# Attention scores in eight array tiles of 32 queries instead of four of 64, and one masked copy instead of two

## The chip, the cores and the metric

The kernel runs on one core of one Trainium2 chip. A core has five engines that work side by side: TensorE (PE, matrix products), VectorE (DVE), ScalarE (ACT), GpSimd (POOL) and SyncE (SP, which here issues the transfers). The metric is the time of one execution on the device in microseconds, as the median of several runs. The kernel before takes 720.04 us, the median of 3 runs (719.09 to 720.98).

## The reference

Four sequences of 768 positions with 8 heads of 64 dimensions go through attention in which a query sees the last 128 positions up to itself (the window) and the first 4 positions of the sequence (the sinks). What comes out goes through a feed-forward block of 2048 hidden units.

```python
scores = scale * np.matmul(q, k.transpose(0, 1, 3, 2))
rel = pos[:, None] - pos[None, :]
in_window = (rel >= 0) & (rel < int(window))
keep = is_sink | in_window
scores = np.where(keep, scores, -1000000000.0)
scores = scores - np.max(scores, axis=-1, keepdims=True)
a = np.exp(scores)
a = a / (np.sum(a, axis=-1, keepdims=True) + 1e-09)
return np.matmul(a, v).astype(np.float32)
# then, on all 3072 rows of 512:
h = x @ w_in
sp = np.maximum(h, 0.0) + np.log1p(np.exp(-np.abs(h)))
g = h * erf(sp)
return (g @ w_out).astype(np.float32)
```

## The kernel before, in words

The work is cut into 12 groups of 256 queries (three a sequence), and a group's attention into four steps, one for each pair of heads: 48 steps, numbered s. A group's 256 queries are two blocks of 128, i = 0 and 1. The feed-forward block of a group (lines 761 to 822) runs as 16 blocks f of 128 hidden units; its matmuls fill PE while the attention of later groups is worked in between.

A step goes through these stages: `load` and `prep` bring queries and keys into `kq` with the 64 dimensions of head 0 on partitions 0 to 63 and those of head 1 on partitions 64 to 127; `score` (lines 369 to 428) makes the exponentials; `norm` divides by the sums; `ptrans`, `pread` and `phalf` turn the probabilities round (from step 15 on by way of DVE's transpose and DRAM) and POOL cuts them into halves by the diagonal (line 522); `av` (line 563) multiplies with the values; `xfin` copies out.

In `kq` a row holds, for a pair of heads, three stretches of 144 columns (`KB` = 128 keys of a block and 16 columns for the sinks): the previous block, block 0 and block 1; then the two blocks of queries. A query of block i needs the end of the previous block's keys, the sinks, and the beginning of its own block's. So a contiguous run of columns of `kq`, beginning in the previous block and ending in the own one, covers what a set of neighbouring queries sees.

In `score` the queries of a block are taken in two halves of 64 (`lo`, `hi`). For each half and each head there is one float32 matmul (line 404) of 64 dimensions by 64 queries by 208 keys (`lo`) or 224 keys (`hi`). The float32 matmul is two passes on PE, each with a load of its weights and a record of its own. Two heads lie in the two row halves of the array and write two PSUM banks; two halves of the queries lie in its two column halves and write the two halves of the partitions. Where a group is the first of its sequence, block 0 has no previous block and its runs are 144 columns.

The runs are put into the bank so that the own block's key t stands `KB` columns (or, for `hi`, a like distance) beside the previous block's key t. Of these two a query sees exactly one, as the window is 128 long. Two predicated copies on DVE (line 417), one for `lo` and one for `hi`, each over both heads and both blocks, copy the own block's scores over the previous block's under a triangle `tri` of 64 x 64. After that 144 columns hold all that the softmax needs; a custom DVE operation (line 422) adds the mask and takes the minimum of the negated scores, ScalarE makes the exponential (line 426).

The order of work is not fixed by the loops alone. Every piece is emitted with a priority (`at`, the offsets in `O`), and a planner with a cost model writes out each engine's queue from priorities and modelled times; `follow` ties two instructions of one engine in order. The matmuls of one `score` call are tied one behind another, and from step 17 on the scores follow the attention output of step s - 2 in one burst. A feed-forward block's projection onto the output comes `LAG` = 4 blocks after its hidden layer and activation.

The bank for the scores comes from the pool `ps_s`, which has one buffer of two banks; step 1 uses `ps_h` tiles, step 2 `ps_o` tiles.

Of the kernel before, what the change touches and what calls it, by code (L numbers as in the profile page):

```python
# [9 lines left out]
F32 = mybir.dt.float32  # L10
# [4 lines left out]
ALU = mybir.AluOpType  # L15
# [4 lines left out]
P = 128  # L20
# [19 lines left out]
NE, AL = 4, 2  # L40
# [22 lines left out]
def kernel(  # L63
# [11 lines left out]
    nc = tc.nc  # L75
# [11 lines left out]
    KB, S3 = P + SW, 6 * SW  # L87
# [31 lines left out]
    def set_flags(behind):  # L119
# [3 lines left out]
        behind(nc.vector.tensor_scalar(flag[:, 3:4], eff[0:1, 1:2], float(P), None, op0=ALU.is_le))  # L123
        nc.vector.tensor_reduce(flag1, flag, axis=AX.X, op=ALU.min)
        nc.vector.tensor_copy(flagi, flag1)
# [12 lines left out]
    def fast_path():  # L138
        with ExitStack() as st:
            pers = st.enter_context(tc.tile_pool(name="pers", bufs=1))  # L140
# [7 lines left out]
            ps_s = st.enter_context(tc.tile_pool(name="ps_s", bufs=1, space=PSUM))  # L148
# [6 lines left out]
            rf = work.tile([P, 512], F32, tag="u", bufs=UB, name="rf")  # L155
# [25 lines left out]
            set_mask(mask0)  # L181
            set_mask(mask1)

            tri = pers.tile([P, 64], mybir.dt.int8, name="tri")
            nc.vector.tensor_scalar(tri[:64], rf[:64, :64], float(P), None, op0=ALU.is_ge)
            nc.vector.tensor_scalar(tri[64:], rf[64:, 64:128], float(P), None, op0=ALU.is_lt)

# [6 lines left out]
            sinks = dram.tile([B * NPAIR, P // 2, 2, 2, D], F32, tag="sinks", bufs=1, name="sinks")  # L196

            pst = pers.tile([P, RING, 2, 2, KB], F32, name="pst")

            xp, early = {}, {}  # L200

# [5 lines left out]
            lo, hi = slice(0, HP), slice(HP, P)  # L207
# [122 lines left out]
            def follow(prev, ins):  # L330

                if prev is not None:
                    tc.add_manual_dep(
                        ins.ins, prev.ins.name,
                        mybir.DependencyInfo(mybir.DependencyClass.NoSync, mybir.DependencyReason.DATA), reason="order",
                    )
                return ins
# [22 lines left out]
            def core(s):  # L360

                prev = mark.get(("p", s - 1)) if s - AL == 3 * NPAIR - 1 else None
                late = s - AL >= 2 * NPAIR and s - AL != 3 * NPAIR - 1
                if late:
                    prev = av(s - AL)
                if s < NSTEP:
                    score(s, prev)

            def score(s, prev):

                g, c = divmod(s, NPAIR)
                gb = g % GPB
                d = stp[s]
                d["sum"] = small.tile([P, 2, 2], F32, tag="sum", name=f"sum_{s}")
                d["neg"] = small.tile([P, 2, 2], F32, tag="neg", name=f"neg_{s}")

                ps, both = [], None
                for h in range(2):
                    nm = f"ps_{s}_{h}"
                    if s == 1:  # L380
                        ps.append(ps_h.tile([P, 2, GT], F32, tag="h", name=nm).rearrange("p a t -> p (a t)"))
                    elif s == 2:
                        ps.append(ps_o.tile([P, DM], F32, tag="o", name=nm))
                    else:
                        if both is None:
                            both = ps_s.tile([P, 2, 512], F32, tag="s", name=f"ps_{s}")
                        ps.append(both[:, h, :])


                dx = KB + 80  # L390
                X = [80, 80 + dx]
                for i in range(2):
                    qt = kq[:, c, 3 + i, :]
                    kt = kq[:, c].rearrange("p n t -> p (n t)")
                    runs = ((lo, KB * i, KB + 64, X[i]), (hi, KB * i + 64, KB + 80, X[i] - 80))
                    if gb + i == 0:
                        runs = ((lo, KB, KB, X[i]), (hi, KB, KB, X[i]))
                    for hf, r0, n, x in runs:
                        for h in (1, 0):
                            r = slice(64 * h, 64 * h + 64)  # L400
                            with at(pos(s), "rest") if s >= TT + AL else nullcontext():
                                prev = follow(
                                    prev,
                                    nc.tensor.matmul(ps[h][hf, x : x + n], qt[r, hf], kt[r, r0 : r0 + n], start=True, stop=True),
                                )

                i0 = int(gb == 0)
                for hf, x, y in ((lo, X[0], X[0] + KB), (hi, X[0] + 64, X[0] - 80)):
                    for t in (both,) if both is not None else ps:
                        t = t if both is not None else t.rearrange("p (h t) -> p h t", h=1)  # L410
                        n = t.shape[1]
                        o, w = (
                            t[hf, :, z : z + 2 * dx].rearrange("p h (i t) -> p h i t", i=2)[:, :, i0:, e : e + 64]
                            for z, e in ((min(x, 64), x - min(x, 64)), (min(y, 64), y - min(y, 64)))
                        )
                        mk = tri[hf].rearrange("p (a b t) -> p a b t", a=1, b=1).broadcast_to([64, n, 2 - i0, 64])
                        nc.vector.copy_predicated(o, mk, w)
                for i in range(2):
                    mk = mask if gb > 0 else (mask0, mask1)[i]
                    for h in range(2):  # L420
                        y = pst[:, s % RING, i, h, :]
                        mark["t", s] = nc.vector.tensor_tensor_reduce(  # L422
                            out=y, in0=ps[h][:, X[i] : X[i] + KB], in1=mk, scale=-scale, scalar=3.0e38, op0=ALU.add, op1=ALU.min,
                            accum_out=d["neg"][:, i, h : h + 1],
                        )
                        mark["e", s] = nc.scalar.activation(  # L426
                            y, y, AF.Exp, bias=d["neg"][:, i, h : h + 1], scale=-1.0, accum_out=d["sum"][:, i, h : h + 1]
                        )
# [155 lines left out]
            def at(a, what):  # L584

                key = int(a * PW) + O[what] + (E.get(what, 0) if a < EA else 0)
                return tc.high_priority(offset=tc.tile_snap_priority() + 1 - key)

            def pos(s):

                return s if s < NE else 3 * s - 6 if s < 2 * NPAIR else 4 * s - 12

            plan = {}
            for s in range(NSTEP + AL):
# [23 lines left out]
                if s < 2 * NPAIR:  # L618
                    x = pos(s) + (3 if s < NE else 5)
# [22 lines left out]
            for n in range(32):  # L642
                x = n - 16
# [68 lines left out]
            for m in range(-LEAD, NG * NF + LAG + 2):  # L712
                a = m + LEAD
                live = 0 <= m < NG * NF
                if live:
                    g, f = divmod(m, NF)
# [6 lines left out]
                w = m - LAG  # L723
                if 0 <= w < NG * NF:
# [3 lines left out]
                    if f2 == NF - 1:  # L728
                        for i in range(2):
                            r0 = (g2 * 2 + i) * P  # L730
# [93 lines left out]
    def general_path():  # L824

        NT_S = S // P
        with ExitStack() as st:
# [7 lines left out]
            with tc.tile_pool(name="g_one0", bufs=1) as one, tc.tile_pool(name="g_work0", bufs=2) as work:  # L835
# [16 lines left out]
                with tc.For_i(0, B * H, 1) as bh:  # L852
# [14 lines left out]
                    for i in range(NT_S):  # L867
# [14 lines left out]
                        mx = work.tile([P, 2], F32, tag="mx", name=f"g_mx{i}")  # L882
                        nc.vector.tensor_reduce(mx[:, 0:1], p, axis=AX.X, op=ALU.max)
                        nc.vector.tensor_scalar_mul(mx[:, 0:1], mx[:, 0:1], -1.0)
# [14 lines left out]
            with tc.tile_pool(name="g_one1", bufs=1) as one, tc.tile_pool(name="g_work1", bufs=2) as work:  # L899
# [3 lines left out]
                with tc.For_i(0, B, 1) as b:  # L903
                    for gb in range(GPB):
# [25 lines left out]
                        for i in range(2):  # L930
# [3 lines left out]
                            )  # L934

    fast_path()
    ok = nc.values_load(flagi[0:1, 0:1], min_val=0, max_val=1)
    with tc.If(ok == 0):
# [31 lines left out]
```

## Time and profile before

| | |
|---|---|
| median of 3 runs | 720.04 us (719.09 to 720.98) |
| the profiled execution | 719.41 us, span 717.4 us |
| PE busy | 689.5 us (96%), 5515 passes |
| PE weight loads busy | 568.2 us (79%) |
| DVE busy | 549.4 us (77%) |
| ACT busy | 493.6 us (69%) |
| POOL busy | 299.1 us (42%) |
| granted PE clock, mean | 0.993 |

The span runs from the first to the last instruction of the profiled execution; the execution's own time is a little more. Busy times of PE are those of overlapping passes, so a busy PE may still be waiting for its own pipeline. Rows of the trace name a group of instructions by the line of the kernel, the engine, the operation, and the tile written and read (`ps<-kq`); `x16` is a count.

### The profile page before, as it was taken

Reading aid. Unit: us, or ns where it says so; the run is one execution under the profiler, and the core shown is the slowest. Engines: PE = TensorE matmul, PEld = TensorE weight load, DVE = VectorE, ACT = ScalarE, POOL = GpSimd, SP = SyncE. Lnnn points to the kernel's source line nnn. Section 1 sums busy time; section 2 is a strip of 40 time slices with the busy share of each in tenths; the row PEclk is TensorE's granted clock in tenths of the full one; section 3 lists DMA queues with packets and bytes.
Section 4 is the critical chain, followed back from the end, with each engine's and each line's share of the span. In section 5 each row is a group of like instructions: output and inputs, shape, how many; then the busy total and the mean of one; then the engine's idle time right before and its main releaser. Section 6 shows DMA issues by size and latency. Waiting matters only on the chain. (4 is left out here: it accounts for less than half of the span.)

```text
span 717.4 us, 16155 instructions
## 1 busy us (share of the span) xinstructions
PE 689.5 (96%) x5515; PEld 568.2 (79%) x5515; DVE 549.4 (77%) x1473; ACT 493.6 (69%) x1157; POOL 299.1 (42%) x501
## 2 busy tenths in 40 slices
PE   6779999999999999999999999999999999999997
PEld 3566557688887888788788888888888888889885
DVE  6979997687789888788888588688698687754352
ACT  4777676986984867476677586586677577586572
POOL 3412400234444546454554444555554437342221
PEclk9999999999999999999999999999999999999999
DMA  6999410302216454543553363463463543220001
GB/s 159 283 320 344 168 27 5 78 16 46 66 34 118 102 117 100 127 104 72 124 118 72 65 135 74 87 136 75 95 124 72 102 96 71 44 68 1 30 1 35
DMA packets 246858, 70.10 MB, mean 98 GB/s; under 512 B 214704, under 2 KB 238896, under 8 KB 246768
## 3 DMA queue, kind: packets, MB, share of 16 engines
q1 hardware_dynamic: 246208, 68.92, 41.1%
q8 instruction: 46, 0.75, 0.4%
q14 instruction: 44, 0.36, 0.2%
q10 hardware_dynamic: 560, 0.07, 0.1%
HBM read 50.27 MB, written 18.42 MB: 96 GB/s over the span
## 5 line engine op out<-in xcount | busy, mean ns | idle before, releaser
L770 PE MATMUL h<-xh,wt 128*128 128x256 f32 x1408 | 275.1, 284 | 0.8 <-DVE u L792 0.7
L770 PEld LDWEIGHTS h<-xh,wt 128*128 128x128 f32 x1408 | 223.7, 188 | 15.4 <-issue 8.2
L770 PE MATMUL h<-xl,wt 128*128 128x256 f32 x704 | 197.3, 281 | 0.0
L800 POOL TENSOR_TENSOR g<-u,g 128x512 fp32r<-128x512 f32 x84 | 113.9, 1356 | 181.3 <-DVE g L799 160.1
L788 ACT ACTIVATE u<-r 128x512 f32<-128x512 f32 x288 | 163.1, 622 | 19.2 <-DMA out_dram<-ot 5.3
L792 DVE SCALAR_TENSOR_TENSOR u<-u,u 128x512 f32<-128x512 f32 x168 | 136.6, 813 | 14.0 <-ACT u L788 1.6
L770 PEld LDWEIGHTS h<-xl,wt 128*128 128x128 f32 x704 | 132.1, 188 | 7.0 <-issue 2.8
L815 PE MATMUL o<-wt,g 128*128 128x512 f32 x336 | 134.1, 399 | 0.5 <-DVE g L799 0.5
L816 PE MATMUL o<-wt,g 128*128 128x512 f32 x336 | 132.8, 395 | 0.0
L817 PE MATMUL o<-wt,g 128*128 128x512 f32 x336 | 129.8, 397 | 0.6 <-POOL g L800 0.4
L426 ACT ACTIVATE pst<-pst,neg 128x144 f32<-128x144 f32 x192 | 77.4, 405 | 61.0 <-DVE neg L422 60.7
L792 DVE SCALAR_TENSOR_TENSOR u<-u,h 128x512 f32<-128x512 f32 x84 | 56.8, 676 | 54.9 <-ACT u L788 53.1
L783 ACT ACTIVATE r<-h 128x512 f32<-128x512 f32 x96 | 56.8, 592 | 51.0 <-PE h L770 42.8
L522 POOL TENSOR_SCALAR_AFFINE_SELECT pz<-pa 64x256 f32<-64x256 f32 (+1 forms) x96 | 47.1, 491 | 70.0 <-ACT pa L484 68.9
L815 PEld LDWEIGHTS o<-wt,g 128*128 128x128 f32 x336 | 63.0, 187 | 14.6 <-ACT u L788 1.3
L817 PEld LDWEIGHTS o<-wt,g 128*128 128x128 f32 x336 | 61.7, 187 | 16.0 <-POOL g L800 1.4
L816 PEld LDWEIGHTS o<-wt,g 128*128 128x128 f32 x336 | 63.0, 188 | 10.8 <-issue 0.3
L785 ACT ACTIVATE r<-r 128x512 f32<-128x512 f32 x96 | 60.6, 631 | 2.8
L784 ACT ACTIVATE r<-r 128x512 f32<-128x512 f32 x96 | 60.6, 631 | 2.6
L799 DVE CAST g<-u 128x512 fp32r<-128x512 f32 x84 | 37.4, 445 | 27.3 <-PE o L817 24.1
L513 POOL COPY pz<-pa 64x256 f32<-64x256 f32 x66 | 31.5, 477 | 55.4 <-DMA pa<-pd 54.6
L522 POOL TENSOR_SCALAR_AFFINE_SELECT pa<-pa 64x256 f32<-64x256 f32 (+1 forms) x96 | 50.4, 525 | 4.9
(99 smaller groups left out, 916.6 us busy)
## 6 DMA issues: line engine op xcount, KB each, us to landing
pd<-turn SPq DMA_DIRECT2D x33, 320.0 KB, 2.6
pa<-pd SPq DMA_DIRECT2D x132, 80.0 KB, 2.6
ws<-in_moe_w_in_dram SPq DMA_DIRECT2D x16, 512.0 KB, 6.1
ws<-in_moe_w_out_dram SPq DMA_DIRECT2D x16, 512.0 KB, 8.5
out_dram<-ot SPq DMA_DIRECT2D x24, 256.0 KB, 2.4
v<-in_v_dram SPq DMA_DIRECT2D x56, 96.0 KB, 2.5
kq<-in_k_dram SPq DMA_DIRECT2D x144, 32.0 KB, 2.0
kq<-in_q_dram SPq DMA_DIRECT2D x144, 32.0 KB, 2.2
```

The lines of the kernel that those rows point to most:

```text
L426: mark["e", s] = nc.scalar.activation(y, y, AF.Exp, bias=d["neg"][:, i, h : h + 1], scale=-1.0, accum_out=d["sum"][:, i, h : h + 1])
L522: nc.gpsimd.affine_select(out=out, in_=x, pattern=[[0, 2], [0, 2 - i0], [-sg, HP]], compare_op=op, fill=0.0, base=0, channel_multiplier=sg,)
L770: last = nc.tensor.matmul(o, wt[NC * j + c][:, p, fs], xt[e][:, c, :], start=(m == 0), stop=(m == len(ops) - 1))
L783: nc.scalar.activation(r, h, AF.Tanh, bias=b_t, scale=0.5)
L784: nc.scalar.activation(r, r, AF.Square, bias=b_v, scale=-0.5)
L785: nc.scalar.activation(r, r, AF.Square, bias=b_r)
L788: sq = nc.scalar.activation(u, r, AF.Square, bias=b_a[i], scale=CS)
L792: pr = nc.vector.scalar_tensor_tensor(out=acc, in0=u, scalar=CC[i] * CS**2, in1=x, op0=ALU.add, op1=ALU.mult)
L800: nc.gpsimd.tensor_tensor(gl, acc, gh.bitcast(F32), op=ALU.subtract)
L815: behind(nc.tensor.matmul(o, gh[:, ws], wt[16 + f][:, 0, :], start=(f == 0), stop=False))
L816: nc.tensor.matmul(o, gh[:, ws], wt[16 + f][:, 1, :], start=False, stop=False)
L817: nc.tensor.matmul(o, gl[:, ws], wt[16 + f][:, 0, :], start=False, stop=(f == NF - 1))
```

## The change

The queries of a block are taken in four sets of 32 instead of two of 64, so that a matmul has 64 dimensions, 32 queries and 176 keys (`KB + 32`). A block has eight matmuls instead of four, in eight tiles of the array: two row halves by four column quarters. All sets of a block use one layout in the bank, with the own block's key t always 144 columns behind the previous block's key t; block 1 begins at column 240. Therefore one predicated copy over 128 partitions and 128 columns, under a triangle of 128 x 128, takes the place of the two over 64 partitions. What a set of 32 rows doesn't write is under the copy or outside of the triangle. The bank tile is allocated once for all steps, and in steps 0, 1, 2 and 4 (`NE`) the runs are widened so that no column that the copy reads was never written.

```diff
--- before.py
+++ after.py
@@ -181,9 +181,8 @@
             set_mask(mask0)
             set_mask(mask1)
 
-            tri = pers.tile([P, 64], mybir.dt.int8, name="tri")
-            nc.vector.tensor_scalar(tri[:64], rf[:64, :64], float(P), None, op0=ALU.is_ge)
-            nc.vector.tensor_scalar(tri[64:], rf[64:, 64:128], float(P), None, op0=ALU.is_lt)
+            tri = pers.tile([P, P], mybir.dt.int8, name="tri")
+            nc.vector.tensor_scalar(tri, rf[:, :P], float(P), None, op0=ALU.is_ge)
 
 
 
@@ -196,6 +195,8 @@
             sinks = dram.tile([B * NPAIR, P // 2, 2, 2, D], F32, tag="sinks", bufs=1, name="sinks")
 
             pst = pers.tile([P, RING, 2, 2, KB], F32, name="pst")
+
+            score_banks = ps_s.tile([P, 2, 512], F32, tag="s", name="ps")
 
             xp, early = {}, {}
 
@@ -382,39 +383,40 @@
                     elif s == 2:
                         ps.append(ps_o.tile([P, DM], F32, tag="o", name=nm))
                     else:
-                        if both is None:
-                            both = ps_s.tile([P, 2, 512], F32, tag="s", name=f"ps_{s}")
+                        both = score_banks
                         ps.append(both[:, h, :])
 
 
-                dx = KB + 80
-                X = [80, 80 + dx]
+                X = [0, 240]
                 for i in range(2):
                     qt = kq[:, c, 3 + i, :]
                     kt = kq[:, c].rearrange("p n t -> p (n t)")
-                    runs = ((lo, KB * i, KB + 64, X[i]), (hi, KB * i + 64, KB + 80, X[i] - 80))
-                    if gb + i == 0:
-                        runs = ((lo, KB, KB, X[i]), (hi, KB, KB, X[i]))
-                    for hf, r0, n, x in runs:
+                    for j in range(0, P, 32):
+                        r0, n, x = KB * i + j, KB + 32, X[i] + j
+                        if s in (0, 1, 2, NE):
+                            n = max(n, X[1] + 32 * i - j)
+                        if gb + i == 0:
+                            r0, n, x = KB, KB, X[i]
                         for h in (1, 0):
                             r = slice(64 * h, 64 * h + 64)
                             with at(pos(s), "rest") if s >= TT + AL else nullcontext():
                                 prev = follow(
                                     prev,
-                                    nc.tensor.matmul(ps[h][hf, x : x + n], qt[r, hf], kt[r, r0 : r0 + n], start=True, stop=True),
+                                    nc.tensor.matmul(
+                                        ps[h][j : j + 32, x : x + n], qt[r, j : j + 32], kt[r, r0 : r0 + n], start=True, stop=True
+                                    ),
                                 )
 
                 i0 = int(gb == 0)
-                for hf, x, y in ((lo, X[0], X[0] + KB), (hi, X[0] + 64, X[0] - 80)):
-                    for t in (both,) if both is not None else ps:
-                        t = t if both is not None else t.rearrange("p (h t) -> p h t", h=1)
-                        n = t.shape[1]
-                        o, w = (
-                            t[hf, :, z : z + 2 * dx].rearrange("p h (i t) -> p h i t", i=2)[:, :, i0:, e : e + 64]
-                            for z, e in ((min(x, 64), x - min(x, 64)), (min(y, 64), y - min(y, 64)))
-                        )
-                        mk = tri[hf].rearrange("p (a b t) -> p a b t", a=1, b=1).broadcast_to([64, n, 2 - i0, 64])
-                        nc.vector.copy_predicated(o, mk, w)
+                for t in (both,) if both is not None else ps:
+                    t = t if both is not None else t.rearrange("p (h t) -> p h t", h=1)
+                    n = t.shape[1]
+                    o, w = (
+                        t[:, :, z : z + 2 * X[1]].rearrange("p h (i t) -> p h i t", i=2)[:, :, i0:, e : e + P]
+                        for z, e in ((0, 0), (32, KB - 32))
+                    )
+                    mk = tri.rearrange("p (a b t) -> p a b t", a=1, b=1).broadcast_to([P, n, 2 - i0, P])
+                    nc.vector.copy_predicated(o, mk, w)
                 for i in range(2):
                     mk = mask if gb > 0 else (mask0, mask1)[i]
                     for h in range(2):
```

## Rows read from the trace of the kernel before

**Rows 1.** Busy time by stage: us, PE, PEld, DVE, ACT, POOL (x), PEclk, DMA, GB/s.

```profile
20.00:100.00 80.00, 71.47 (x478) 48.97 (x477) 74.10 (x183) 59.25 (x152) 26.81 (x40) 0.96 0.77 244
100.00:625.00 525.00, 518.57 (x4383) 436.04 (x4383) 421.25 (x1144) 368.90 (x874) 242.37 (x420) 1.00 0.41 85
625.00:717.40 92.40, 87.10 (x571) 75.97 (x569) 39.97 (x70) 55.24 (x95) 23.75 (x21) 0.98 0.09 26
```

**Rows 2.** PE's waits, 100 to 625 us: who waited for whom, us, times, longest.

```profile
PE av L563 <- POOL pa L522: 4.2, 3, 2.8
PE h L770 <- DVE u L792: 0.7, 2, 0.5
PE av L563 <- ACT pa L484: 0.6, 1, 0.6
PE o L815 <- DVE g L799: 0.5, 1, 0.5
...
```

**Rows 3.** PE's timeline around one burst of scores: start, us, engine, line, operation.

```profile
...
240.44 0.99 PE L404 MATMUL ps<-kq 64*64 64x208 f32 x16
241.36 0.38 PE L770 MATMUL h<-xh,wt 128*128 128x256 f32 x1
```

**Rows 4.** That burst in narrow stretches, line 404 alone: PE, PEld, instructions under way (x).

```profile
240.43:240.46 0.03, 0.02 (x4) 0.02 (x4) 1.00 0.19 30
240.46:240.52 0.06, 0.06 (x4) 0.06 (x8) 1.00 0.18 26
240.52:240.66 0.14, 0.14 (x4) 0.12 (x8) 1.00 0.51 85
240.66:240.70 0.04, 0.04 (x8) 0.03 (x3) 1.00 0.68 112
240.84:240.89 0.05, 0.05 (x10) 0.05 (x4) 1.00 0.94 154
241.01:241.08 0.07, 0.07 (x10) 0.01 (x2) 1.00 0.71 112
...
```

**Rows 5.** Groups by shape, 100 to 625 us: count, busy us, mean ns, idle before.

```profile
L770 PEld LDWEIGHTS h<-xh,wt 128*128 128x128 f32 x1200 | 190.8, 188 | 14.6 <-issue 8.2 <-DVE u L792 1.3 <-PE ps L404 1.0
...
L404 PE MATMUL ps<-kq 64*64 64x224 f32 x270 | 34.6, 360 | 0.0
L404 PE MATMUL ps<-kq 64*64 64x208 f32 x268 | 32.2, 347 | 0.0
...
L404 PEld LDWEIGHTS ps<-kq 64*64 64x64 f32 x634 | 21.3, 132 | 4.5 <-issue 0.7
...
L404 PE MATMUL ps<-kq 64*64 64x144 f32 x96 | 5.7, 308 | 0.0
```

**Rows 6.** PE's timeline, scores of a sequence's first group.

```profile
...
208.08 0.85 PE L404 MATMUL ps<-kq 64*64 64x144 f32 x16
208.86 0.55 PE L563 MATMUL av<-pa,v 128*64 128x128 f32 x8
...
```

**Rows 7.** Line 404 alone by stage: us, PE (x), PEld (x).

```profile
...
100.00:625.00 525.00, 39.76 (x634) 21.27 (x634) 1.00 0.41 85
...
```

**Rows 8.** Groups by shape over the span: DVE's copies and its mask operation.

```profile
L422 DVE CUSTOM_DVE_ANT_0 pst<-ps,mask 128x144 f32<-128x144 f32 x192 | 47.6, 304 | 1.5
...
L417 DVE COPY_PREDICATED ps<-tri,ps 64x256 f32<-64x256 int8 x64 | 27.5, 430 | 2.4
...
L417 DVE COPY_PREDICATED ps<-tri,ps 64x128 f32<-64x128 int8 x28 | 8.3, 296 | 0.9
...
L417 DVE COPY_PREDICATED ps<-tri,ps 64x64 f32<-64x64 int8 x8 | 1.5, 228 | 2.7 <-PE ps L404 2.6
```

**Rows 9.** DVE's timeline behind the burst of rows 3.

```profile
...
242.50 0.42 DVE L417 COPY_PREDICATED ps<-tri,ps 64x256 f32<-64x256 int8 x1
242.84 0.68 DVE L792 SCALAR_TENSOR_TENSOR u<-u,u 128x512 f32<-128x512 f32 x1
...
```

**Rows 10.** Busy time of a stretch of attention output, scores, attention output; columns as rows 1.

```profile
207.13:209.81 2.68, 2.68 (x65) 2.21 (x65) 1.61 (x3) 2.14 (x5) 0.44 (x2) 1.00 0.46 81
...
```

## Prediction

> **What bounds the kernel now.** I read the busy times by stage first [rows 1]. From 100 to 625 us TensorE (PE) is busy 518.57 of 525 us, VectorE (DVE) 421.25, ScalarE 368.90; no other engine comes near. From 20 to 100 us the DMA engines are 77% busy and PE 71.47 of 80 us. After 625 us no scores are left. The second view is PE's waits in the 525 us [rows 2]: the four largest entries come to 6.0 us in seven waits, 4.2 of them for POOL's halves of the probabilities and 1.2 for DVE. So in this stage what PE is given to do, with what lies between its instructions, sets the time, and a shorter burst on PE moves everything behind it forward. The end of the kernel is PE's too: the tail holds only the feed-forward matmuls.
>
> The third view is one burst of scores on PE's timeline [rows 3]. Sixteen passes (eight float32 matmuls, each recorded as two passes) begin at 240.44, and the next matmul begins at 241.36: 0.92 us. The busy times of the burst in narrow stretches [rows 4] show what is inside: at 240.46 four matmuls are under way after 0.02 us, none is added until 240.66, four more by 240.70, then again at 240.84 and 241.01. So four passes run at a time (two heads in the two row halves, two query halves in the two column halves), in four rounds: two blocks of queries, two passes each. The rounds are 0.22, 0.18 and 0.18 us apart, and the last needs 0.28 to 0.35 us until another kind of matmul may begin. The longer shape of each round, 224 columns, sets it.
>
> **The change part by part.** *Columns.* All tiles stream 176 columns where the longest had 224. A column's price: 360 and 347 ns for 224 and 208 columns [rows 5] give 13/16 = 0.81 ns; a round of 0.175 us for 208 columns [rows 4] gives 0.84. At 0.83, 48 columns fewer are 40 ns in each of four rounds, the last included, since its drain follows its last column: 160 ns less a burst.
>
> *Twice the passes.* The burst has 32 passes and 32 weight loads for 16 and 16. If all eight tiles of a round run together, the number of rounds stays four, and the price is that the last tile starts later. Four started within 0.02 us [rows 4], at most 7 ns apart; four more at that pace are 27 ns, paid once. The weight loads of the first round lie open: the first round is 0.045 us longer than the others. A load takes 188 ns for 128 columns and 132 for 64 [rows 5], 0.9 ns a column, so 32 columns fewer take back at most 28 ns and at least nothing; I take 13. A full burst: 160 - 27 + 13 = 146 ns (133 to 161).
>
> [...] No row here has eight tiles in flight, though.
>
> *First block of a sequence.* Where the group is the first of its sequence, the first block has 144 columns before and after, so only two rounds shrink: 80 - 27 + 13 = 66 ns (53 to 81). Such a burst takes 0.78 us now [rows 6].
>
> *How many bursts count.* Between 100 and 625 us lie 634 passes [rows 7], 39 bursts of 16 and the rest of one. Their 96 passes of 144 columns [rows 5] are eight in each of 12 bursts; 27 are full. 27 x 0.146 + 12 x 0.066 = 3.9 + 0.8 = 4.7 us less (4.2 to 5.3). All of it is on PE's path. Bursts before 100 us I take at nothing: DMA and the chain of first steps cover them [rows 1]. If that cover isn't there, five bursts give 0.5 us back, against the columns that the change adds in steps 0, 1, 2 and 4 to fill the bank (up to 272 for 224, two rounds each, 0.1 to 0.2 us a step): -0.5 to +0.6 us.
>
> *The copies.* Two predicated copies of 64 x 256 become one of 128 x 512. Its shape isn't in the trace; 228, 296 and 430 ns for 64, 128 and 256 elements [rows 8] grow by 1.05 ns an element, so 698 ns for one against 860 for two, and 430 against 592 at a sequence's start. Twice the partitions cost nothing by the nearest row: 128 x 144 through line 422 takes 304 ns, the copy of 64 x 128 296 [rows 8]. That is 0.16 us a step off DVE, 6 us in the stage, and I count it as nothing, because PE waited for DVE 1.2 us in all [rows 2]. It can also hurt: another operation of DVE now fits between the copies, as the 0.68 us one at 242.84 [rows 9], and behind a single copy such an operation waits up to 0.27 us more. Queued behind it on DVE are the activation's products, for which PE's projections wait; the planner puts a projection four feed-forward blocks behind its activation, which covers that. Bounds: -1.2 us (all of PE's waits for DVE) to +0.5 us (one more wait as long as the longest of these, 0.5).
>
> *One fixed bank tile, one mask operation fewer.* The bank had one buffer before, so a step's matmuls waited for the same readers as now. The mask is built once: nothing. What can move is the order that the planner writes out, since it weighs the new instructions; a PE wait of the longest kind seen, 2.8 us [rows 2], can appear or go. I take 0, with +-2.8 us.
>
> **The sum.** The profiled execution took 719.4 us, 2.0 more than its span. 719.4 - 4.7 = 714.7. The runs' median, 720.04, is 0.6 above it, so the forecast on the runs' scale is 715.3 us.
>
> **The rivals.** *Hidden anyway.* PE arrives earlier and waits longer for POOL's halves, which hang on transfers. For it: the largest wait of PE is this one [rows 2]. Against it: three such waits in 39 bursts, and POOL's input starts from the scores, which come earlier too. The gain shrinks to 0 to 2 us: 718 to 720, or 721 with a wait added; I say 719.
>
> *Only two column strips at a time (slower).* The place is the array's stream of moving columns: no row shows more than two strips of one row half streaming different keys at once [rows 4]. If four strips take turns in twos, the burst has eight rounds of 176 x 0.84 ns = 0.149 us or so: 0.047 (starts) + 0.032 (first load) + 8 x 0.149 + 0.09 (past the last column: 0.28 less 224 x 0.83 ns) = 1.36 us in place of 0.92. At a sequence's start four of the eight are of 144 columns, 0.122 us, and it has 1.25 for 0.78. That is 0.44 x 27 + 0.47 x 12 = 17.5 us more: 738. It decides from where a fifth round is needed, one round being 0.149 us and the gain 0.146. [...]
>
> *Too many instructions for the pace at which PE takes them (slower).* Each round needs 16 records in 0.149 us, 9 ns each. For it: the densest long stretch in the trace, attention output, scores and attention output again, has about 128 records in 2.68 us, 21 ns each [rows 10], and nothing shows more. Against it: that stretch is paced by its columns, and 12 records begin within 0.08 us at the burst's start [rows 4]. At 21 ns, 64 records need 1.34 us and the burst, with 0.24 us for the last round, 1.58: +0.66 x 27 + 0.80 x 12 = +27 us. At the pace of the first 12 records, 7 ns, it costs nothing. [...] The likeliest harm is the small one, a pace somewhat over 9 ns: 11 ns gives 64 x 11 + 240 = 0.94 us, +0.02 x 27 + 0.16 x 12 = +2.5 us: 722.5.
>
> **Chances.** Forecast 0.62 (712.5 to 717.5); hidden 0.21; two strips 0.09; pace 0.08. A measurement of this kernel tells 0.3%, 2.2 us, from no change. Faster by more: the forecast and a little of the hidden case, 0.64. Within: most of the hidden case, 0.19. Slower: both last rivals and the hidden case with a new wait, 0.17. The range 711.5 to 722 takes in the forecast with the planner's wait on the good side, and the hidden case; it leaves out the two strips, the worse part of the pace, and little else, 0.18.
>
> **What would show it.** Right: PE's timeline has 32 passes of 176 columns a burst; the next matmul begins 0.75 to 0.79 us after the first pass, 0.70 to 0.74 at a sequence's start; narrow stretches show eight passes under way within 0.06 us and rounds 0.15 us apart; line 417's successor takes about 0.70 us; PE's waits between 100 and 625 us stay near 6 us. Wrong: more than four rounds (the strips), starts inside a round spread over more than 0.1 us (the pace), or bursts as short as forecast beside PE waits grown by 3 us or more (hidden, or the planner's order).

## The result, and the profile after

The kernel after takes 725.21 us, the median of 9 runs (721.97 to 728.16), against 720.04 us for the kernel before (9 runs): 1.0077 times the time, 95% interval 1.005 to 1.0104. It is slower by about 5 us where 4.7 us less (715.3 us) were forecast. The profiled execution took 724.09 us with a span of 722.3 us. Lines behind the changed ones have moved by one or two: 404 is 405, 417 is 419, 770 is 772, 788 is 790, 792 is 794.

The busy time by stage of the kernel after, with the columns of [rows 1]:

```profile
20.00:100.00 80.00, 70.37 (x516) 48.60 (x516) 72.70 (x175) 57.89 (x150) 27.15 (x40) 0.91 0.75 242
100.00:625.00 525.00, 516.45 (x4969) 433.29 (x4969) 420.86 (x1095) 370.36 (x869) 238.01 (x414) 1.00 0.41 85
625.00:722.30 97.30, 92.00 (x644) 80.77 (x640) 45.22 (x81) 57.45 (x104) 27.08 (x28) 0.99 0.09 27
```

The burst itself did what was forecast. PE's timeline around the burst of [rows 3], in the kernel after:

```profile
241.72 0.64 PE L565 MATMUL av<-pz,vz 128*64 128x64 f32 x16
242.28 0.83 PE L405 MATMUL ps<-kq 64*32 64x176 f32 x32
243.04 0.38 PE L772 MATMUL h<-xh,wt 128*128 128x256 f32 x1
```

It begins at 242.28 and the next matmul at 243.04: 0.76 us where [rows 3] have 0.92. Its narrow stretches, line 405 alone (columns as in [rows 4]):

```profile
242.28:242.31 0.03, 0.03 (x4) 0.03 (x4) 1.00 0.64 102
242.31:242.36 0.05, 0.05 (x8) 0.05 (x16) 1.00 0.62 102
242.36:242.44 0.08, 0.08 (x8) 0.08 (x16) 1.00 0.95 157
242.44:242.51 0.07, 0.07 (x16) 0.07 (x12) 1.00 1.08 176
```

Eight passes are under way within 0.08 us, none is added until 242.44, then eight more. Over the stage a full burst needs 0.757 us on average for 0.917 before, and one at a sequence's start, where no wait follows it, 0.704 for 0.784. Times the 27 and 12 bursts of the prediction that is 27 x 0.160 + 12 x 0.080 = 5.3 us less. The copies, by shape over the span:

```profile
L419 DVE COPY_PREDICATED ps<-tri,ps 128x512 f32<-128x512 int8 x32 | 22.0, 688 | 4.9 <-PE ps L405 4.7
L419 DVE COPY_PREDICATED ps<-tri,ps 128x256 f32<-128x256 int8 x14 | 5.9, 423 | 0.0
```

688 and 423 ns, where 698 and 430 were estimated from [rows 8]. So 5 us came off and some 10 us came on elsewhere. PE's waits from 100 to 625 us (columns as in [rows 2]) show a first part of them:

```profile
PE h L772 <- DVE u L794: 7.6, 8, 3.4
PE o L819 <- POOL g L802: 0.5, 2, 0.3
PE o L817 <- DVE g L801: 0.2, 1, 0.2
```

The waits for POOL's halves that led [rows 2] are gone. In their place the hidden layer waits eight times for the activation `u` of an earlier block, 7.6 us in all and once for 3.4 us. I follow that one back. PE's timeline at the wait (start, us, engine, line, operation, and in brackets the idle time before it and what ended it):

```profile
309.43 0.77 PE L405 MATMUL ps<-kq 64*32 64x144 f32 x32
...
313.57 0.36 PE L772 MATMUL h<-xh,wt 128*128 128x256 f32 x1 [3.37 <-DVE u L794]
```

ScalarE's timeline a few microseconds earlier:

```profile
302.11 1.15 ACT L790 ACTIVATE u<-r 128x512 f32<-128x512 f32 x2
309.46 0.63 ACT L790 ACTIVATE u<-r 128x512 f32<-128x512 f32 x1 [6.20 <-DMA out_dram<-ot]
```

ScalarE stood 6.20 us because `u` and the outgoing rows `ot` share one tag of four buffers, and the transfer that frees the buffer had not been made. SP's timeline says why; first of the kernel after, then of the kernel before:

```profile
302.20 0.96 SPq L242 DMA_DIRECT2D v<-in_v_dram  x2
303.26 1.17 SPq L249 DMA_DIRECT2D vz<-sinks  x2
304.52 1.03 SPq L233 DMA_DIRECT2D kq<-in_k_dram  x2
305.65 0.88 SPq L734 DMA_DIRECT2D out_dram<-ot  x2
306.57 2.04 SPq L233 DMA_DIRECT2D kq<-in_k_dram  x2
```

```profile
300.52 0.96 SPq L241 DMA_DIRECT2D v<-in_v_dram  x2
301.58 0.41 SPq L732 DMA_DIRECT2D out_dram<-ot  x1
302.09 1.18 SPq L248 DMA_DIRECT2D vz<-sinks  x2
303.37 0.54 SPq L732 DMA_DIRECT2D out_dram<-ot  x1
304.00 2.76 SPq L232 DMA_DIRECT2D kq<-in_k_dram  x4
```

Before, the two output transfers of group 3 were issued at 301.58, ahead of the sinks, and at 303.37, behind them, both ahead of all the key loads. After, they stand behind the sinks and two key loads, at 305.65. No line of the diff touches them; the planner wrote SP's queue anew. The stretches around the wait, kernel after, columns as in [rows 1]:

```profile
305.00:310.00 5.00, 4.65 (x84) 4.34 (x84) 1.25 (x3) 0.54 (x1) 2.72 (x7) 1.00 0.57 168
310.00:313.50 3.50, 0.21 (x16) 0.00 (x0) 1.81 (x3) 3.37 (x7) 1.27 (x1) 1.00 0.74 145
313.50:320.00 6.50, 6.42 (x33) 6.05 (x34) 6.12 (x17) 6.31 (x18) 5.32 (x10) 0.74 0.42 82
...
314.80:318.20 3.40, 3.40 (x17) 3.34 (x16) 3.37 (x14) 3.28 (x8) 3.23 (x7) 0.51 0.31 75
```

PE worked 0.21 of 3.50 us, and in the 6.5 us behind that its granted clock is 0.74 on average; in finer stretches it is about half, 0.51, from 314.8 to 318.2, 1.00 from 313.5 to 314.8 and 0.98 from 318.2 to 320. The wait is paid once as idle time and again as slower matmuls: three passes of the hidden layer need 0.64 us at half the clock (315.46 to 316.10) and 0.36 us before (313.77 to 314.13). It is not wholly an extra cost, though. The kernel before has a wait in this place too, 2.83 us for POOL's halves:

```profile
305.99 0.67 PE L563 MATMUL av<-pa,v 128*64 128x128 f32 x12 [2.83 <-POOL pa L522]
```

There the granted clock stayed at 1.00 from 300 to 315 us.

The second part is in PE's own queue. The burst of step 8, kernel after:

```profile
104.80 0.52 PE L405 MATMUL ps<-kq 64*32 64x176 f32 x14
105.25 0.33 PE L565 MATMUL av<-pz,vz 128*64 128x64 f32 x2
105.51 0.48 PE L405 MATMUL ps<-kq 64*32 64x176 f32 x2
105.93 0.33 PE L565 MATMUL av<-pz,vz 128*64 128x64 f32 x2
106.18 0.48 PE L405 MATMUL ps<-kq 64*32 64x176 f32 x2
...
109.54 0.50 PE L405 MATMUL ps<-kq 64*32 64x176 f32 x6
109.97 0.66 PE L352 MATMUL tqk<-ident,kq 128*128 128x128 f32 x4
```

The scores are not in one burst: after the first 14 passes the attention output comes between them two passes at a time, and each pair (two passes of either kind) needs 0.67 us. The 32 passes take from 104.80 to 109.97. Of the other early steps, 1, 2, 4, 5, 7 and 9 are split as well; in the kernel before only step 8 was. In step 5, PE then waits 2.16 us in the middle of its scores for DVE.

### The profile page after: what moved, and what is told of

Read it like the earlier page. It is cut to its first block, busy times and chain, and to the rows that moved or that the text cites. A ratio compares the mean times of both kernels' runs of the same rounds, so it can differ in the third digit from the quotient of the medians.

```text
span 722.3 us, 17632 instructions
## 1 busy us (share of the span) xinstructions
PE 691.7 (96%) x6283; PEld 569.3 (79%) x6283; DVE 552.1 (76%) x1422; ACT 495.6 (69%) x1157; POOL 298.6 (41%) x501
## 5 line engine op out<-in xcount | busy, mean ns | idle before, releaser
L772 PE MATMUL h<-xh,wt 128*128 128x256 f32 x1408 | 277.9, 287 | 7.8 <-DVE u L794 7.6
L772 PE MATMUL h<-xl,wt 128*128 128x256 f32 x704 | 199.4, 283 | 0.0
L790 ACT ACTIVATE u<-r 128x512 f32<-128x512 f32 x288 | 164.3, 623 | 34.8 <-DMA out_dram<-ot 11.2
L802 POOL TENSOR_TENSOR g<-u,g 128x512 fp32r<-128x512 f32 x84 | 115.7, 1377 | 152.9 <-DVE g L801 147.0
L794 DVE SCALAR_TENSOR_TENSOR u<-u,u 128x512 f32<-128x512 f32 x168 | 150.4, 895 | 18.0 <-ACT u L790 5.4
L524 POOL TENSOR_SCALAR_AFFINE_SELECT pz<-pa 64x256 f32<-64x256 f32 (+1 forms) x96 | 52.7, 549 | 59.9 <-ACT pa L486 58.7
L443 DVE TENSOR_SCALAR pst<-pst,sum 128x128 f32<-128x128 f32 x168 | 50.8, 364 | 1.5
```

The source lines that it names most:

```text
L524: nc.gpsimd.affine_select(out=out, in_=x, pattern=[[0, 2], [0, 2 - i0], [-sg, HP]], compare_op=op, fill=0.0, base=0, channel_multiplier=sg,)
L772: last = nc.tensor.matmul(o, wt[NC * j + c][:, p, fs], xt[e][:, c, :], start=(m == 0), stop=(m == len(ops) - 1))
L790: sq = nc.scalar.activation(u, r, AF.Square, bias=b_a[i], scale=CS)
L794: pr = nc.vector.scalar_tensor_tensor(out=acc, in0=u, scalar=CC[i] * CS**2, in1=x, op0=ALU.add, op1=ALU.mult)
L802: nc.gpsimd.tensor_tensor(gl, acc, gh.bitcast(F32), op=ALU.subtract)
```

## The experiments

The theory after this reading: the new tiles gain about 5 us, and the planner's new order of the queues loses about 10. The rival: the eight tiles cost something on the chip that the burst's timeline doesn't show. To tell them apart, a helper chained the instructions of an engine one behind another in a recorded order, without adding a semaphore, so that the same work could run in either order. Every run is compared with the kernel before on the same chip; it had medians of 718.87, 719.29 and 718.80 us on the three chips used. Differences between two changed kernels are taken from the ratios, times 719 us; each ratio is uncertain by 1.4 to 2.2 us.

### The same work in the other's order

```diff
+            def arrange(code, only=None):
...
+                for en, keys in plan_of.items():
...
+                    for key in keys:
+                        for x in per[en, key]:
+                            if prev is not None:
+                                tc.add_manual_dep(
+                                    x, prev.name,
+                                    mybir.DependencyInfo(mybir.DependencyClass.NoSync, mybir.DependencyReason.DATA), reason="order",
+                                )
+                            prev = x
...
+            arrange(ORDER)
```

*The kernel after, all queues in the order of the kernel before*, with step 8's burst whole:

> The changed kernel (eight tiles, one copy), with every engine's queue held in the order that the planner wrote out for the kernel before. Theory (the time is lost in the planner's new order, above all the output transfers behind key loads on SP at 303 us and the order of the first 60 us; the burst itself gains): bursts stay 0.757 and 0.704 us, PE waits between 100 and 625 us fall back from some 7.6 to about 6 us, and the time is 720.0 - 5.3 (27 x 0.160 + 12 x 0.080) = about 715 us, ratio 0.991 to 0.995. Rival (eight tiles cost time in the hardware: clock, instruction supply, the single long copy): the order changes nothing, 724 to 726 us, ratio 1.005 to 1.010.

Measured 710.23 us, ratio 0.9884 (0.9856 to 0.9911), faster than the theory's range. *The kernel before in the order of the kernel after*, its bursts whole:

> The kernel before (four tiles, two copies), with every queue held in the order that the planner wrote out for the changed kernel. Theory (order): it has the changed kernel's stalls without the gain of the bursts, 725.2 + 5.3 = about 730 us, ratio 1.010 to 1.016, with PE waiting some 3 us for DVE near 310 us behind a late output transfer. Rival (hardware cost of eight tiles): this kernel has none of it, about 720 us, ratio 0.998 to 1.002.

Measured 725.64 us, ratio 1.0093 (1.0072 to 1.0115), a little below the theory's range. The order decides the sign with either set of tiles: four tiles lose in the new order, eight gain in the old one. The rival falls. *Only SP's queue in the old order*, the other engines ordered by the planner (`arrange(ORDER, ('EngineType.SP',))`):

> The changed kernel with SP's queue alone (the transfers) held in the old order; the other engines are ordered by the planner. Theory: the stall of 3.4 us near 310 us and the half clock behind it (3.4 us at half speed, 1.7 us) go, the loss of the first 60 us (about 4 us) stays as far as it isn't SP's: 719 to 722 us, ratio 0.998 to 1.003. If the transfers' order is all of it: 715 us. Rival (hardware): 724 to 726 us.

Measured 715.96 us, ratio 0.9966 (0.9943 to 0.9988): 1.11% or 8.0 us faster than the kernel after. This isn't the order of the transfers alone. With SP's queue given, the planner wrote the other queues anew: PE's departs from that of the kernel after by its 361st pass, at 44 us, and step 7's burst is whole. What SP's order alone is worth this run can't say. *One copy without the eight tiles*, in the old order, step 8 whole:

```diff
-                    for j in range(0, P, 32):
-                        r0, n, x = KB * i + j, KB + 32, X[i] + j
+                    for j in range(0, P, 64):
+                        r0, n, x = KB * i + j, KB + 64, X[i] + j
...
-                                        ps[h][j : j + 32, x : x + n], qt[r, j : j + 32], kt[r, r0 : r0 + n], start=True, stop=True
+                                        ps[h][j : j + 64, x : x + n], qt[r, j : j + 64], kt[r, r0 : r0 + n], start=True, stop=True
```

> Four tiles of 64 queries in the new layout (208 columns each, none of 224) with the one copy of 128 x 512, in the old order of all queues. It separates the copy from the tiles. Rounds of 208 for 224 columns give 4 x 13 ns a full burst and 2 x 13 at a sequence's start: 27 x 0.052 + 12 x 0.026 = 1.7 us. Theory (order is what costs, the copy is free): 718 us, ratio 0.996 to 0.999, PE bursts of 0.865 us. Rival (the one long copy holds up DVE): slower than before, 722 us or more.

Measured 712.99 us, ratio 0.9924 (0.9902 to 0.9945), better than I expected. The runs whose PE followed a recorded order kept step 8's burst whole, which the order of before did not; how much that is worth had to be known.

### Controls: what the whole burst of step 8 is worth

*The kernel before in its own order, step 8's burst whole:*

> The kernel before, unchanged in its work, held in its own order with one difference, which the two kernels of old order e1 and e4 had too: the burst of step 8, into which the planner had put 7 foreign matmuls (6.06 us from its first pass to the next matmul), runs whole. It is the control that e1 and e4 lacked. Theory (that split burst costs PE time between 98 and 108 us, and e1's 8.6 us are 5.3 of the bursts and the rest of this): 3 to 5 us less than before, ratio 0.993 to 0.996. Rival (the copy and the tiles gave e1 all of it): no change, ratio 0.999 to 1.001.

Measured 717.13 us, ratio 0.9976 (0.9952 to 1.0): 1.7 us, less than the 3 to 5 expected and at the edge of what can be told from nothing. *The kernel after in exactly the order of the kernel before*, step 8 split as there:

> The changed kernel in exactly the old order, with the burst of step 8 split as it was. What is left of the change is the eight tiles and the one copy. Theory: 27 x 0.160 + 12 x 0.080 = 5.3 us less than before, ratio 0.991 to 0.994. Rival (the copy gives as much again, as e4's 5.9 us seem to say): 8 to 9 us less, ratio 0.987 to 0.989.

Measured 713.97 us, ratio 0.9921 (0.989 to 0.9951): -5.7 us by the ratio. This is the change without the planner's part, and it agrees with the 5.3 us worked out from the bursts. Against the first run it makes step 8's split worth 0.37%, 2.7 us, where the first control has 1.7. The one copy with four tiles gained 0.52% on the first control, 3.7 us, where the columns alone give some 1.7 (16 fewer in each of four rounds in 27 bursts and of two rounds in 12, at 0.83 ns); with intervals of nearly 2 us on either ratio I can't tell whether the copy gives the rest.

### The two places, mended one at a time

Both keep the order that the planner wrote for the kernel after in every queue, but for the edit. *The two output transfers of group 3 moved up on SP:*

```diff
 SP, around group 3's outputs
-  v v  vz vz  kq kq  out out  kq kq
+  v v  out  vz vz  out  kq kq  kq kq
```

> The changed kernel in its own new order but for two transfers: on SP the two output tiles of group 3 stand where the old order has them, ahead of the key loads and round the first copies of the sinks. Theory (a late output keeps a buffer from ScalarE, PE waits 3.4 us for DVE and then runs 3.4 us at half clock): 725 - 3.4 - 1.7 = 720 us, no wait of PE over 1 us near 310 us, ratio 0.999 to 1.004. Rival (the stall moves to the next wait, or was covered by something else late): 724 to 726 us, ratio 1.006 to 1.010.

Measured 721.17 us, ratio 1.0024 (1.0004 to 1.0045): 0.53%, 3.8 us faster than the kernel after. SP's timeline and ScalarE's wait, of this kernel:

```profile
303.04 0.41 SPq L922 DMA_DIRECT2D out_dram<-ot  x1
303.55 1.18 SPq L433 DMA_DIRECT2D vz<-sinks  x2
304.82 0.54 SPq L922 DMA_DIRECT2D out_dram<-ot  x1
```

```profile
305.62 0.63 ACT L980 ACTIVATE u<-r 128x512 f32<-128x512 f32 x1 [2.16 <-DMA out_dram<-ot]
```

```profile
PE h L962 <- DVE u L984: 6.0, 8, 1.4
```

ScalarE waits 2.16 us for 6.20, and PE's longest wait for `u` falls from 3.4 to 1.4 us. *The seven split bursts made whole on PE:*

```diff
 PE, step 8 (as in steps 1, 2, 4, 5, 7 and 9)
-  S x14  av x2  S x2  av x2  S x2 ... av x2  S x6
+  S x32  av x14
```

> The changed kernel in its own new order with its seven split bursts (steps 1, 2, 4, 5, 7, 8, 9) whole. Theory (split bursts of the first 120 us cost PE time, the stall near 310 us stays): 2 to 5 us less than the changed kernel, 720 to 723 us, ratio 1.001 to 1.006. Rival (splitting costs nothing, the first 100 us are bound by transfers and the chain of first steps): 724 to 726 us.

Measured 719.17 us, ratio 0.9996 (0.9973 to 1.0019): 0.81%, 5.8 us, a little more than expected. The four tiles in this same order, their bursts whole too, had 1.0093: here the eight tiles and the one copy are worth 0.97%, 7.0 us, and between the two kernels of the old order with whole bursts 0.92%, 6.6 us. PE's timeline at step 8, of this kernel:

```profile
103.27 0.28 PE L734 MATMUL av<-pz,vz 128*64 128x64 f32 x2
103.48 0.83 PE L571 MATMUL ps<-kq 64*32 64x176 f32 x32
104.24 0.68 PE L734 MATMUL av<-pz,vz 128*64 128x64 f32 x14
104.85 0.66 PE L517 MATMUL tqk<-ident,kq 128*128 128x128 f32 x4
```

The same matmuls take 1.4 us, from 103.48 to 104.85, where they took 5.2. *Both edits together:*

> The changed kernel in its own new order with both repairs: the seven bursts of steps 1 to 9 whole (as c4) and the two outputs of group 3 up (as c3). Theory (two separate places, so their gains add): 725.2 - 4.1 - 6.0 = 715 us, ratio 0.992 to 0.997, with the step of c4 before 120 us and that of c3 near 310 us both to be seen in how far PE has come. Rival (one repair takes what the other gave): 718 to 720 us.

Measured 715.09 us, ratio 0.9943 (0.9923 to 0.9963): the two add up, 9.6 us. Where the rest of the way to the first run lies is seen in PE's progress, worked out from the traces: the time in us at which the k-th matmul of the hidden layer (2240 in all) begins.

| k | before | after | outputs up | bursts whole | both | SP old | all old, whole |
|---|---|---|---|---|---|---|---|
| 64 | 64.93 | 67.56 | 67.45 | 66.35 | 66.13 | 65.70 | 63.58 |
| 128 | 107.78 | 110.38 | 110.26 | 105.26 | 105.05 | 105.46 | 101.46 |
| 768 | 294.29 | 295.66 | 295.87 | 289.84 | 291.14 | 295.21 | 288.30 |
| 832 | 320.15 | 322.70 | 317.41 | 316.13 | 312.35 | 316.63 | 314.96 |
| 1600 | 536.56 | 541.64 | 537.24 | 533.75 | 530.57 | 531.55 | 528.33 |

The whole bursts give their 5 us before 110 us, the outputs theirs between the 768th and the 832nd. There the outputs' edit does better than the old order itself: 21.5 us with the outputs up, 27.0 in the kernel after, 25.9 before and 26.7 with all queues in the old order. The old order waits in this place for POOL's halves, as the kernel after in exactly the old order shows (PE's waits, columns as in [rows 2]):

```profile
PE av L754 <- POOL pa L713: 2.4, 2, 2.2
```

So the two outputs explain only a part of what separates the two orders. From the 832nd to the 1600th the kernel with both edits needs 218.2 us, the one with all queues in the old order 213.4, and the one with SP's queue in the old order, the others planned anew, 214.9. By this count, which leaves out PE's other matmuls, nearly 5 us more of the new order's cost lie between 312 and 540 us. Which queue and which instructions it is I didn't try.

### Without a recorded order

Can the gain be had from the planner? *The rule that kept a burst together in the later steps, for all steps:*

```diff
-                            with at(pos(s), "rest") if s >= TT + AL else nullcontext():
+                            with at(pos(s), "rest") if s >= TT + AL or i + j + 1 - h else nullcontext():
```

> The changed kernel, ordered freely by the planner, with one line changed: the second to last matmuls of a burst get the raised priority 'rest' in all steps, not from step 17 on. All bursts come out whole, the two outputs of group 3 stay behind the key loads. Theory (whole bursts are what c4 gained): 718 to 721 us, ratio 0.998 to 1.003. Rival (a free planner gives the gain back elsewhere): 723 us or more.

Measured 718.15 us, ratio 0.9991 (0.9971 to 1.0011). *With it, the outputs issued from ScalarE's queue in place of SP's:*

```diff
-                                nc.sync.dma_start(out[r0 : r0 + P, :], mlp.result(g2, i))
+                                nc.scalar.dma_start(out[r0 : r0 + P, :], mlp.result(g2, i))
```

> p1 with the output transfers issued from ScalarE's queue, where the copy that makes the tile runs just before, instead of SP's. No load can stand ahead of them. Theory (late outputs keep ScalarE's buffers and so PE waiting): 3 to 6 us less than p1, 713 to 717 us, ratio 0.991 to 0.997, and ScalarE's waits for the outputs fall from some 11 us to about 5 or less. Rival (issuing costs ScalarE as much, or the planner's order shifts again): as p1 or slower.

Measured 711.47 us, ratio 0.9887 (0.9862 to 0.9912). ScalarE's waits for the outputs' buffers over the span (us, times, longest), in the kernel after, with the first edit, and with both:

```profile
ACT u L790 <- DMA out_dram<-ot: 11.2, 8, 6.2
```

```profile
ACT u L790 <- DMA out_dram<-ot: 11.5, 7, 4.8
```

```profile
ACT u L790 <- DMA out_dram<-ot: 6.3, 8, 2.0
```

The first edit takes the splits away and leaves these waits. The second nearly halves them (6.3 us, where about 5 were expected), and the kernel is 7.5 us faster than with the first alone, more than the 3 to 6 expected. In both the planner also wrote other queues anew, PE's and ScalarE's among them, so the gain needn't be that of the outputs alone. *Four tiles of 64 queries and one copy* (the edit of the fourth run), the planner left to itself:

> Four tiles of 64 queries in the new layout with the one copy, ordered freely by the planner. In that order only step 8's burst is split, as before the change, and the two outputs of group 3 stand behind two copies of the sinks and two key loads. Theory (splitting comes with the eight tiles, the late outputs with the copy): before - 1.7 + some 4 for the stall near 310 us = 720 to 723 us, ratio 1.000 to 1.005, PE waiting over 2 us near 310 us. Rival (the late outputs come with the eight tiles alone): 717 to 719 us.

Measured 714.82 us, ratio 0.9952 (0.9932 to 0.9972): both expectations missed. With four tiles the planner splits step 8 alone. The outputs of group 3 stand behind the sinks and two key loads here too, and ScalarE waits 2.9 us for their buffer, yet PE's longest wait for `u` between 100 and 625 us is 1.0 us. So an order that costs 10 us came with the eight tiles, and neither with the one copy nor with the fixed bank, which this kernel has too; late outputs alone don't make it. Why the planner weighs 32 instructions otherwise than 16 was not tried.

## Why the prediction was wrong

- **Bound and burst: right.** Forecast were 146 ns off a full burst and 66 off a short one (133 to 161, 53 to 81), measured 160 and 80, at the upper end: the columns' 160 came off whole, as if the 27 ns set against later starts were paid back by the shorter weight loads (132 ns for a 64 x 64 load in [rows 5], 106 for 64 x 32 in the same stretch of the kernel after). The kernel after in exactly the old order is 5.7 us faster than before, where 4.7 were forecast.
- **Copies: right**, 688 ns against 698. Whether they are worth anything stays open.
- **The step that failed** stands under "One fixed bank tile": "What can move is the order that the planner writes out ... I take 0, with +-2.8 us." The same work in the two orders is 11.2 us apart (1.0077 against 0.9921), so the term is mis-sized by a factor of four. Two edits of the new order show what is in it: 3.8 us go with the place of the outputs of group 3 (not all of them lost against the old order, which waits in that stretch too), and some 3.1 with the splits beyond step 8's (5.8 for all seven, less the 2.7 that step 8's cost in the old order too). The 4.2 left between the kernel with both edits and the one with all queues in the old order (0.9943 against 0.9884) are not traced to a place: by the table the first is 3.6 us behind at the 128th matmul of the hidden layer, 2.6 ahead at the 832nd and 2.2 behind at the 1600th. That the three come to 11.1 is no further evidence, since the last is only what the others leave over. My bound took the longest wait of PE as the price of one mishap. It left out that a wait of PE can be followed by a stretch at half the clock (here 3.4 us at 0.51 behind the wait of 3.4 us), that a new order changes many places, and that queues of which the diff says nothing, SP's among them, are written anew.
- **Bursts before 100 us: the reason was wrong.** I set them between -0.5 and +0.6 us, "DMA and the chain of first steps cover them". With the splits mended, PE reaches the 128th matmul of the hidden layer 5.1 us earlier (110.38 to 105.26), and that stays to the end: what PE saves there is not covered. What the shorter bursts save there by themselves was not told apart. The prediction's own terms give five bursts 0.65 us (four of 0.146 and one of 0.066), not 0.5.
- **The rivals.** *Hidden anyway* falls: with the old order all of it shows. *Two column strips* falls: eight passes at a time, in four rounds. *Pace* falls: 32 passes with their loads took 0.757 us, where 21 ns a record would have needed 1.58 us and 11 ns 0.94. No rival named the queue order as a slower case with a price; it stood only among the signs of being wrong, though it was the one step whose size nothing in the profile bounded.

## What to carry to other kernels

Where a planner or a scheduler writes the queues, a change of instruction counts is two changes: the work and the order. Look at both orders side by side before the time is put down to the work, and run the new work in the old order once. Buffers that are freed by a transfer deserve a look at what that transfer stands behind in its queue: here two output transfers behind sinks and key loads were followed by a wait of 3.4 us on PE and by half the clock for as long, and moving them gave 3.8 us; in another order a like place cost PE 1.0 us at most. A burst that pays because it is one needs a rule that keeps it one from the first step on.

## What the runs showed of the hardware

- Eight tiles of 64 x 32 stream at once, two row halves by four column quarters: in the burst at 242.28 of the kernel after, the first eight passes start within 47 ns, 7 ns apart on average, and the rounds of 176 columns are 0.17, 0.15 and 0.15 us apart. Twice the instructions cost the burst nothing visible: 32 passes need 0.757 us, where 16 of 208 and 224 columns needed 0.917.
- Going to and fro between tile shapes cost time here. In the split burst of step 8 two passes of 128 x 64 tiles and two of 64 x 32 need 0.67 us; inside the whole runs of the kernel with whole bursts the same four need some 0.14 (0.76 us for 32 passes of the one, 0.61 for 14 of the other). From these, my estimate is a good 0.25 us a change ((0.67 - 0.14) / 2); what the time goes into the traces don't show.
- After the idle 3.4 us in the kernel after (to 313.57) the granted clock was 1.00 for 1.2 us more and then 0.51 for 3.4 us. The length of the last wait doesn't tell whether it falls: in the kernel before it stayed at 1.00 behind 2.83 us of waiting (from 305.99 to 315), and it fell at 24.8 us behind waits of 1.13 us each (to 22.83 and to 24.61). In the first 56 us it fell to half for 6.8 us twice in the kernel after (0.50 from 24.7 to 31.5 and from 48.6 to 55.4) and for 3.4 us twice in the kernel before (0.51 from 24.8 to 28.2, 0.50 from 48.7 to 52.1); from 36 to 52 us, which takes in the beginning of the second fall, PE was busy 9.79 of 16 us in the kernel after and 12.06 in the kernel before.
